# A seven-product stage: VectorE's sum of two banks ahead of a low part, 24 fill matmuls in every unit, and other places for some steps

## The chip, the cores and the metric

The kernel runs on one core of a Trainium2 chip. TensorE (PE in the profile) multiplies into PSUM, VectorE (DVE) and ScalarE (ACT) do the elementwise work, SyncE (SP) issues nearly all the transfers, and GpSimd (POOL) does almost nothing here. Each engine takes its instructions in the order in which they are written. The metric is the device time of one execution in microseconds, as the median of several.

## The reference

Three layers follow each other on 4 x 3072 = 12288 rows of 256 channels:

```python
scores = (1/S) * z @ z.T;  x = u * (relu(scores)**2 @ v)        # z: 64 columns, S = 3072
h = x @ w_in;              x = (h - tanh(h)) @ w_out            # 256 -> 2048 -> 256
xk, xr = a mix of each row of x with the row before it
out = sigmoid(xr @ w_r) * (relu(xk @ w_k)**2 @ w_v)             # 256 -> 1024 -> 256
```

## The kernel before

**Number format.** Every fp32 operand of a matmul is split into a high part (a rounded copy, type fp32r) and a low part (the operand less its high part). A product of two such operands is three matmuls: high by high, high by low, low by high (`PASSES`). `copy_hi` makes a high part on ScalarE, `sub_lo` a low part on VectorE.

**Stages.** The rows are cut into 24 tiles of 512. The program has three stages: A (attention, 24 x 12 units), S (the middle layer, 96 units) and K (the last layer). TensorE runs all of it; the other engines prepare operands and take results out of PSUM.

**Stage S.** Two tiles of rows are taken together as a chunk; there are 12 chunks of 8 units. A unit computes h for two blocks of 128 of the 2048 columns and for both tiles of rows, as a 2x2 block product in seven multiplications instead of eight. The blocks of w_in are A11, A12, A22 and their sums S1 to S4; the blocks of x are B11, B21, B22 and their differences T1 to T4. The seven products go into the two PSUM banks `e` and `a` of a tile `w_H`; there are two such tiles, used in turn. A product is 3 matmuls of 128x512, a unit 21. Between the products `h_unit` puts "fill" matmuls of the second multiplication (by w_out), which belong to an earlier unit and come from a list `q`, in three runs:

1. A11·B11 and A12·B21. ScalarE copies bank `a` (`r`, L628), VectorE adds bank `e` to it (L698). ScalarE makes the high part `h_Hy` of the unit before, VectorE its low part `l_Hy`.
2. Run 1 of the fill. Then S2·T2 and S1·T1. ScalarE copies both banks (`rc`, L628).
3. Run 2 of the fill, then steps that prepare weights or the next chunk's x (`run_steps`). Then high and low part `h_Hx`, `l_Hx` (`h_split`), the products S4·B22 and S3·T3, and VectorE's sum of both banks with the swapped copy (`rc`, L717). Tanh (L632) and h - tanh(h) (L635) follow.
4. Run 3 of the fill. Then -A22·T4 into bank `a`, which the sum L717 has read before. Its tanh is the last step.

The cuts of the list are `len(q) * 8 // 24` and `len(q) * 15 // 24`, so 24 entries go in runs of 8, 7 and 9. `h_queue(n)` lists what the unit after n multiplies. It lists 18 matmuls for the second unit of a chunk, 30 for the first one, and 24 for the others. In the second unit's list the first entries use `h_Hy` and `l_Hy`, which that unit itself makes. At a chunk's end `x2_out` copies four banks of results out (ScalarE, L739).

**Steps.** `run_steps` takes steps from a list of tasks with due units; each step has a cost, and a unit of stage S gives 1.6 to it. What is overdrawn is taken from the next units' budgets. `x_steps(i)` prepares chunk i: four differences T1 to T4 (in two steps of two, L369), the high and low parts of B11 and B21 (one step), of B22, and of T1 to T4. It may start five units before its chunk.

Of the kernel before, what the change touches and what calls it, by code (L numbers as in the profile page):

```python
# [7 lines left out]
F32 = mybir.dt.float32  # L8
# [11 lines left out]
def relu2_attention__tanh_ffn__channel_mix_kernel(  # L20
# [24 lines left out]
    B, S, D = u.shape  # L45
# [5 lines left out]
    NT = B * NG  # L51
# [310 lines left out]
    def x_steps(i):  # L362

        st = {}
        x = xs[i] = {}

        def minus(n, a, b):
            st[n] = t = p2(f"xd{i}_{n}")
            nc.vector.tensor_tensor(out=t, in0=a, in1=b, op=ALU.subtract)  # L369

        def first():
            a, b = [t.bitcast(F32) for t in xraw[i]]
            minus("T1", b[:, 0], a[:, 0])
            minus("T3", b[:, 1], b[:, 0])

        def second():
            a, b = [t.bitcast(F32) for t in xraw[i]]
            minus("T2", b[:, 1], st["T1"])
            minus("T4", st["T2"], a[:, 1])

        def own(k):
            w = xraw[i][k]
            if k:
                copy_hi(w[:, 0], w[:, 1].bitcast(F32))
                sub_lo(w[:, 1], w[:, 1].bitcast(F32), w[:, 0])
                x["B22"] = (w[:, 0], w[:, 1])
            else:
                h = p4(f"xh{i}", F32R)
                copy_hi(h, w.bitcast(F32))
                sub_lo(w, w.bitcast(F32), h)  # L390
                x["B11"], x["B21"] = (h[:, 0], w[:, 0]), (h[:, 1], w[:, 1])

        def part(n):
            t = st.pop(n)
            if i % 2:
                w = sb.tile([P, 2, 512], F32R, tag="e", name=f"xo{i}_{n}", bufs=5)
            else:
                w = p4(f"xo{i}_{n}", F32R)
            copy_hi(w[:, 0], t)
            sub_lo(w[:, 1], t, w[:, 0])  # L400
            x[n] = (w[:, 0], w[:, 1])

        return [(1.3, first), (1.3, second), (1.3, lambda: own(0))] + [
            (0.7, lambda n=n: part(n)) for n in ("T2", "T1")
        ] + [(0.7, lambda: own(1))] + [(0.7, lambda n=n: part(n)) for n in ("T3", "T4")]

# [224 lines left out]
    def tanh(g, h):  # L631
        nc.scalar.activation(out=g, in_=h, func=ACTF.Tanh)  # L632
# [29 lines left out]
    def h_queue(n):  # L662

        i, j = divmod(n, NHF)
        q = h_piece(n - 1, 1, 0) if j else []
        if j == 0:
            return h_piece(n, 0, 1) + h_piece(n, 1, 1) + h_piece(n, 0, 0)
        q += h_piece(n, 0, 0) + h_piece(n, 0, 1) + h_piece(n, 1, 1)
        if j == NHF - 1:
            q += [lambda: x2_out(i, 1)] + h_piece(n, 1, 0) + [lambda: x2_out(i, 0)]  # L670
        return q

    def h_split(which):

# [10 lines left out]
    def h_unit(n, q):  # L685

        i, j = divmod(n, NHF)
        if "g" not in hb:
            g = sb.tile([P, 2, 2, 512], F32, tag="big", name="g_H", bufs=12)
            hb["g"] = [g[:, 0], g[:, 1]]  # L690
        gx, gy = hb["g"]
        cuts = [len(q) * 8 // 24, len(q) * 15 // 24]
        w = work(f"w_H{n}")
        e, a = w[:, 0], w[:, 1]
        product(a, i, j, "A11", "B11", True, False)
        product(e, i, j, "A12", "B21", True, True)
# [12 lines left out]
        rc = copied(scratch(f"rc_{n}"), w)
        for f in q[cuts[0] : cuts[1]]:  # L710
            f()
        run_steps(NA + n)
        hb["x"] = (n, 0 if n else 1, 2, ((n - 1, 1, 0) if n else None, (n, 0, 0)), gx)
        h_split("x")()
        product(e, i, j, "S4", "B22", False, True)
        product(a, i, j, "S3", "T3", False, False)
        nc.vector.tensor_tensor(out=swapped(rc), in0=w, in1=swapped(rc), op=ALU.add)  # L717
        tanh(gy, rc)
        less(gy, rc)
        hb["y"] = (n, 0, 2, ((n, 1, 1), (n, 0, 1)), gy)  # L720
        for f in q[cuts[1] :]:
            f()
        product(a, i, j, "-A22", "T4", False, True)
        tanh(gx[:, 0], a)
        hb["a"] = a
# [9 lines left out]
    def x2_out(i, t):  # L735
        o = acc.pop(("H", 2 * i + t))
        for c in range(DC):
            x = p2(f"x2_{2 * i + t}_{c}")
            nc.scalar.activation(out=x, in_=o[:, c], func=ACTF.Copy)  # L739
            nc.sync.dma_start(out=x2d[2 * i + t][:, c], in_=x)  # L740
            nc.gpsimd.tensor_copy(edge[:, 2 * i + t, c : c + 1], x[:, TB - 1 :])
# [151 lines left out]
        pieces(last + n, min(last + n + 4, NA - 1), 0, k)  # L893
    weights(last + 8, NA, "out", 0)
    weights(NA, NA, "out", 2)
    for k in range(4):
        pieces(NA + k // 2 + 1, NA + 3, 1, k)
    weights(NA + 3, NA + 4, "out", 1)
    weights(NA + 4, NA + 4, "out", 3)
    n = NB - NHF  # L900
    weights(n + 2, n + 3, "r", 0)
# [18 lines left out]
    def run_steps(n):  # L920

        for x in [x for x in tasks if x[1] <= n]:
            tasks.remove(x)
            ready.append((x[0], list(x[3](*x[4]))))
        ready.sort(key=lambda x: x[0])
        kind = units[min(n, len(units) - 1)][0]
        left = {"A": 2.0, "S": 1.6, "K": 2.4, "R": 4.0}[kind] + spare[0]
        if kind == "A":
            t, q = divmod(n, NP)
            j = pairs[t % NG][q] // 2 - t % NG  # L930
            left -= 0.3 if later(n) else 1.0 if j < 0 else 1.1 if j > 0 else 0.0
        while ready and (left > 0 or ready[0][0] <= n):
            for x in list(ready):
                if left > 0 or x[0] <= n:
                    cost, f = x[1].pop(0)
                    f()
                    left -= cost
                    if not x[1]:
                        ready.remove(x)
        spare[0] = min(left, 0.0)  # L940

    with tc.manual_schedule():
        z_load(0, 0)
# [12 lines left out]
        for m, src in ((0, moe2_mu_k), (1, moe2_mu_r)):
            with nc.allow_non_contiguous_dma(reason="a column of the mixing vector"):
                nc.sync.dma_start(out=mu[:, m, :], in_=src.rearrange("(c p) -> p c", p=P))
        def begin(n):
            for f in loads.pop(n, ()):  # L960
                f()
            if n in stores:
                stores.pop(n)()

        for n in range(NA):
            begin(n)
            produce(units[n])
# [58 lines left out]
```

## Time and profile before

| what | value |
|---|---|
| median of 3 runs | 2650.04 us (2649.84 to 2650.11) |
| the profiled execution | 2651.18 us |
| its span, from the first to the last instruction | 2649.1 us |
| instructions in it | 29587 |
| mean granted TensorE clock | 0.991 of full speed |
| busy share of PE, DVE, ACT | 97%, 72%, 60% |

The span is what the trace covers; 2.08 us of the profiled time lie outside it. Matmuls are pipelined: one of 128x512 is shown with some 0.39 us, but the next one starts after 0.23 us, so that two overlap and a window counts those at both of its edges. Weight loads (PEld) run beside matmuls. Units of stage S are named here by their place in the chunk, j = 0 to 7, and matmuls within a unit by their place from its first product, k = 0, 1, ...

### The profile page before, as it was taken

To read this page: it belongs to the slowest core of one execution; us is meant where nothing else is said; L and a number is where in the kernel's file an instruction comes from. 1 tells how busy PE (TensorE), PEld (TensorE's weight loads), DVE (VectorE), ACT (ScalarE), POOL (GpSimd) and SP (SyncE) were. 2 spreads that over 40 slices of the span, in tenths; PEclk is the share of its full clock that TensorE was granted. 3 is DMA by queue.
4 is the path that set the end of the run, shared out by engine and by line. 5 is a ranking of instruction groups with operands and counts; after the bars stand their busy time and mean duration, and the time that the engine had idled before them with its cause. 6 is when DMAs were issued, how large, how long until landed. Compare 5 with 4: busy or idle time off the path is not lost.

```text
span 2649.1 us, 29587 instructions
## 1 busy us (share of the span) xinstructions
PE 2561.3 (97%) x11051; PEld 2082.9 (79%) x11051; DVE 1896.0 (72%) x2363; ACT 1585.6 (60%) x1973; POOL 15.9 (1%) x53
## 2 busy tenths in 40 slices
PE   9999999999999988999999999999998999999999
PEld 7888888888888877777777777777777788888887
DVE  8888888887788676666766676666666666766765
ACT  7766865776687655555555555555555545544553
POOL 0000000000000000000000000000000000000000
PEclk9999999999999999999999999999999999999999
DMA  7798689579868920000000000000010112121121
GB/s 193 224 232 210 200 230 231 178 215 223 209 228 259 219 96 32 1 32 32 1 32 32 32 1 32 32 32 1 32 60 9 48 42 46 40 47 41 43 46 32
DMA packets 382784, 260.17 MB, mean 98 GB/s; under 512 B 263984, under 2 KB 337712, under 8 KB 382640
## 3 DMA queue, kind: packets, MB, share of 16 engines
q1 hardware_dynamic: 379472, 257.89, 35.7%
q8 instruction: 86, 1.41, 0.2%
q10 hardware_dynamic: 3168, 0.39, 0.1%
q14 instruction: 58, 0.48, 0.1%
HBM read 142.87 MB, written 109.31 MB: 95 GB/s over the span
## 4 chain that ended last, share of the span: by engine, by line
PE 79%; DVE 10%; ACT 7%; DMA 1%; issue 1%; SPq 0%; ACTq 0%; DVEq 0%
PE acc_A L607 28%; PE w_H L622 14%; PE acc_H L655 10%; PE w_K L544 10%; PE acc_K L607 10%; DVE rc L717 3%; PE w_A L521 3%; PE w_A L520 3%; DVE l_Hx L90 3%; PE w_R L559 2%; ACT rc L628 2%; ACT h_Hx L87 1%; DVE xd_T L369 1%; DVE g_H L635 1%; ACT x L739 1%
## 5 line engine op out<-in xcount | busy, mean ns | idle before, releaser
L607 PE MATMUL acc_A<-h_A,v 128*128 128x512 f32 x1344 | 440.0, 389 | 0.8 <-DVE h_A L431 0.8
L622 PE MATMUL w_H<-xo_T,w_in 128*128 128x512 f32 x1152 | 327.5, 407 | 36.8 <-DVE rc L717 35.7
L607 PE MATMUL acc_A<-h_t,v 128*128 128x512 f32 x960 | 309.8, 389 | 0.0
L622 PEld LDWEIGHTS w_H<-xo_T,w_in 128*128 128x128 f32 x1152 | 218.2, 194 | 109.7 <-DVE rc L717 66.0
L655 PE MATMUL acc_H<-h_Hy,w_out 128*128 128x512 f32 x768 | 273.8, 400 | 23.9 <-ACT h_Hy L87 23.9
L607 PEld LDWEIGHTS acc_A<-h_A,v 128*128 128x128 f32 x1344 | 252.2, 188 | 53.7 <-DVE h_A L431 1.2
L427 ACT ACTIVATE a_A<-w_A 128x1024 f32<-128x1024 f32 (+1 forms) x169 | 172.7, 1022 | 198.8 <-PE w_A L521 198.1
L607 PE MATMUL acc_A<-l_A,v 128*128 128x512 f32 x672 | 261.8, 390 | 2.3 <-DVE l_A L90 2.3
L632 ACT ACTIVATE g_H<-rc 128x1024 f32<-128x1024 f32 x96 | 101.8, 1061 | 257.6 <-DVE rc L717 257.6
L655 PE MATMUL acc_H<-h_Hx,w_out 128*128 128x512 f32 x768 | 254.1, 389 | 0.0
L607 PE MATMUL acc_K<-h_K,w_v 128*128 128x512 f32 x768 | 251.8, 389 | 0.0
L544 PE MATMUL w_K<-mkh,w_k 128*128 128x512 f32 x768 | 249.0, 390 | 0.0
L90 DVE TENSOR_TENSOR l_A<-a_A,h_A 128x1024 fp32r<-128x1024 f32 (+1 forms) x169 | 201.9, 1194 | 65.7 <-ACT h_A L87 64.8
L427 ACT ACTIVATE a_K<-w_K 128x1024 f32<-128x1024 f32 x96 | 98.2, 1023 | 225.2 <-PE w_K L544 225.2
L455 DVE STREAM_TRANSPOSE k<-a_A 128x512 f32<-128x512 f32 x240 | 156.0, 689 | 76.4 <-ACT a_A L428 75.8
L607 PEld LDWEIGHTS acc_A<-h_t,v 128*128 128x128 f32 x960 | 180.2, 188 | 37.4
L635 DVE TENSOR_TENSOR g_H<-rc,g_H 128x1024 f32<-128x1024 f32 x96 | 117.7, 1226 | 114.2 <-ACT g_H L632 114.2
L90 DVE TENSOR_TENSOR l_Hx<-g_H,h_Hx 128x1024 fp32r<-128x1024 f32 (+1 forms) x97 | 117.6, 1212 | 113.2 <-ACT h_Hx L87 113.2
L431 DVE CAST h_K<-a_K 128x1024 fp32r<-128x1024 f32 x96 | 66.5, 693 | 184.3 <-ACT a_K L428 181.5
L628 ACT ACTIVATE rc<-w_H 128x1024 f32<-128x1024 f32 x96 | 98.7, 1028 | 163.4 <-PE w_H L622 163.4
L655 PEld LDWEIGHTS acc_H<-h_Hy,w_out 128*128 128x128 f32 x768 | 148.6, 194 | 59.8 <-ACT h_Hy L87 29.0
L607 PE MATMUL acc_A<-l_t,v 128*128 128x512 f32 x480 | 186.7, 389 | 0.0
(154 smaller groups left out, 5081.7 us busy)
## 6 DMA issues: line engine op xcount, KB each, us to landing
at<-k SPq DMA_DIRECT2D x120, 512.0 KB, 3.6
b<-at SPq DMA_DIRECT2D x240, 256.0 KB, 6.3
vr<-in_v_dram SPq DMA_DIRECT2D x24, 512.0 KB, 7.1
uin<-in_u_dram SPq DMA_DIRECT2D x192, 64.0 KB, 2.7
x1d<-x SPq DMA_DIRECT2D x24, 512.0 KB, 3.3
x<-x1d SPq DMA_DIRECT2D x24, 512.0 KB, 4.7
x2d<-x SPq DMA_DIRECT2D x48, 256.0 KB, 2.3
x<-x2d SPq DMA_DIRECT2D x24, 512.0 KB, 3.3
```

The lines of the kernel that those rows point to most:

```text
L90: nc.vector.tensor_tensor(out=o, in0=i, in1=hi.bitcast(F32), op=ALU.subtract)
L427: nc.scalar.activation(out=a[:, x], in_=w[:, x], func=ACTF.Relu, scale=sc)
L455: nc.vector.transpose(out=t[:, :, :, c].rearrange("p b a j -> p a b j"), in_=a[:, c].rearrange("p (a b i) -> p a b i", a=4, b=4),)
L520: nc.tensor.matmul(w[:, j], lhsT, z1[b, g], start=True, stop=False)
L521: nc.tensor.matmul(w[:, j], lhsT, z2[t], start=False, stop=True)
L544: nc.tensor.matmul(w[:, j], ws["k", f // 4][a][:, c, (f % 4) * P : (f % 4 + 1) * P], x[m][:, c], start=n == 0, stop=n == 3 * DC - 1,)
L607: nc.tensor.matmul(o[c], w[j][a][:, c * P : (c + 1) * P], s[m][:, j], start=p == 0 and j == 0 and n == 0, stop=p == last and j == 1 and n ...
L622: nc.tensor.matmul(o, w[l][:, (j % 4) * P : (j % 4 + 1) * P], x[m], start=first and k == 0, stop=last and k == 2, skip_group_check=True,)
L628: nc.scalar.activation(out=t, in_=a, func=ACTF.Copy)
L632: nc.scalar.activation(out=g, in_=h, func=ACTF.Tanh)
L635: nc.vector.tensor_tensor(out=g, in0=h, in1=g, op=ALU.subtract)
L655: nc.tensor.matmul(o[c], ws["out", f // 4][a][:, f % 4, c * P : (c + 1) * P], hp[n, half, t][m], start=bool(first and k == 0), stop=bool(l ...
```

## The change

The sum of both banks (L717) is written ahead of the low part `l_Hx`. The fill is cut at 6 and 14 of 24, so in runs of 6, 8 and 10. The lists of the first two units of a chunk are filled up to 24: the last six matmuls of a chunk move into the second unit of the next one, and `x2_out` is called from the list, one tile in the first unit and one in the second. The first unit of the stage gets 18, since six of its 24 move to the second. The differences T1 to T4 become four steps, a unit's budget falls from 1.6 to 1.4, and the weight pieces of the first chunk get other units.

```diff
-        def first():
-            a, b = [t.bitcast(F32) for t in xraw[i]]
-            minus("T1", b[:, 0], a[:, 0])
-            minus("T3", b[:, 1], b[:, 0])
...
+        def sums():
+            b21, b11, b22, b12 = raw()
+            return [
+                (0.7, lambda: minus("T1", b12, b11)),
+                (0.7, lambda: minus("T3", b22, b12)),
+                (0.7, lambda: minus("T2", b22, st["T1"])),
+                (0.7, lambda: minus("T4", st["T2"], b21)),
+            ]
...
-        return [(1.3, first), (1.3, second), (1.3, lambda: own(0))] + [
+        return sums() + [(1.3, lambda: own(0))] + [
...
     def h_queue(n):
 
         i, j = divmod(n, NHF)
-        q = h_piece(n - 1, 1, 0) if j else []
+        q = h_piece(n - 1, 1, 0) if n else []
         if j == 0:
-            return h_piece(n, 0, 1) + h_piece(n, 1, 1) + h_piece(n, 0, 0)
-        q += h_piece(n, 0, 0) + h_piece(n, 0, 1) + h_piece(n, 1, 1)
+            if n:
+                q[-1] = with_out(q[-1], i - 1, 0)
+            return q + h_piece(n, 0, 1) + h_piece(n, 1, 1) + h_piece(n, 0, 0)
         if j == NHF - 1:
-            q += [lambda: x2_out(i, 1)] + h_piece(n, 1, 0) + [lambda: x2_out(i, 0)]
-        return q
+            q += h_piece(n, 0, 1) + h_piece(n, 1, 1) + h_piece(n, 0, 0)
+            q[17] = with_out(q[17], i, 1)
+            return q
+        return q + h_piece(n, 0, 0) + h_piece(n, 0, 1) + h_piece(n, 1, 1)
+
+    outs = []
+
+    def with_out(f, i, t):
+        def g():
+            f()
+            outs.append((i, t))
+
+        return g
+
+    def empty():
+        for x in outs:
+            x2_out(*x)
+        outs.clear()
...
-        cuts = [len(q) * 8 // 24, len(q) * 15 // 24]
+        cuts = [len(q) * 6 // 24, len(q) * 14 // 24]
...
-        h_split("x")()
+        low = h_split("x")
+        empty()
         product(e, i, j, "S4", "B22", False, True)
         product(a, i, j, "S3", "T3", False, False)
         nc.vector.tensor_tensor(out=swapped(rc), in0=w, in1=swapped(rc), op=ALU.add)
+        low()
+        for f in q[cuts[1] :]:
+            f()
+        empty()
         tanh(gy, rc)
         less(gy, rc)
         hb["y"] = (n, 0, 2, ((n, 1, 1), (n, 0, 1)), gy)
-        for f in q[cuts[1] :]:
-            f()
...
-    for k in range(4):
-        pieces(NA + k // 2 + 1, NA + 3, 1, k)
-    weights(NA + 3, NA + 4, "out", 1)
+    for k, n in enumerate((NA + 1, NA + 2, NA + 3, NA + 2)):
+        pieces(n, n, 1, k)
+    weights(NA + 4, NA + 4, "out", 1)
...
-        left = {"A": 2.0, "S": 1.6, "K": 2.4, "R": 4.0}[kind] + spare[0]
+        left = {"A": 2.0, "S": 1.4, "K": 2.4, "R": 4.0}[kind] + spare[0]
...
         q = [f for u in units[NA - LAG : NA] for f in pieces_of(u)]
-        q += [f for cost, f in x1_steps(NT - 1)]
+        rest = q[-6:] + [f for cost, f in x1_steps(NT - 1)]
+        q = q[:-6]
         for n in range(NS):
             begin(NA + n)
             h_unit(n, q)
-            q = h_queue(n)
+            q = rest + h_queue(n)
+            rest = []
+        q += h_piece(NS - 1, 1, 0)
+        q[-1] = with_out(q[-1], NT // 2 - 1, 0)
```

First place, VectorE in unit 26 (j = 2 of a chunk); `l_Hy25` belongs to the unit before. Before:

```order
L698 TENSOR_TENSOR r1_26_10273<-w_H26_10266,r1_26_10273 128x512
L635 TENSOR_TENSOR g_H_8381<-w_H25_10200,g_H_8381 128x512
L90 TENSOR_TENSOR l_Hy25_10277<-g_H_8381,h_Hy25_10276 128x1024
L635 TENSOR_TENSOR g_H_8381<-r1_26_10273,g_H_8381 128x512
L90 TENSOR_TENSOR l_Hx26_10307<-g_H_8381,h_Hx26_10306 128x1024
L717 TENSOR_TENSOR rc_26_10297<-w_H26_10266,rc_26_10297 128x2x512
L635 TENSOR_TENSOR g_H_8381<-rc_26_10297,g_H_8381 128x1024
```

And now, with the lines of the changed file (L718, L638 and L738 are the old L698, L635 and L717):

```order
L718 TENSOR_TENSOR r1_26_10273<-w_H26_10266,r1_26_10273 128x512
L638 TENSOR_TENSOR g_H_8379<-w_H25_10186,g_H_8379 128x512
L90 TENSOR_TENSOR l_Hy25_10277<-g_H_8379,h_Hy25_10276 128x1024
L638 TENSOR_TENSOR g_H_8379<-r1_26_10273,g_H_8379 128x512
L738 TENSOR_TENSOR rc_26_10295<-w_H26_10266,rc_26_10295 128x2x512
L90 TENSOR_TENSOR l_Hx26_10306<-g_H_8379,h_Hx26_10305 128x1024
L638 TENSOR_TENSOR g_H_8379<-rc_26_10295,g_H_8379 128x1024
```

The sum `rc_26` and the low part `l_Hx26` have changed places. Second place, TensorE between the second and the third product of the same unit, `xo3_T2` and `xo3_T1` being T2 and T1 of its chunk. Before:

```order
L622 MATMUL w_H26_10266<-xh3_9871,w_in0_0_7415 128x512
L655 MATMUL acc_H6_10251<-h_Hx25_10237,w_out2_8418 128x512
L655 MATMUL acc_H6_10251<-l_Hx25_10238,w_out2_8418 128x512
L655 MATMUL acc_H6_10251<-h_Hx25_10237,w_out2_8418 128x512 x2
L655 MATMUL acc_H6_10251<-l_Hx25_10238,w_out2_8418 128x512
L655 MATMUL acc_H6_10251<-h_Hx25_10237,w_out2_8418 128x512
L655 MATMUL acc_H6_10251<-h_Hx25_10237,w_out0_8374 128x512
L655 MATMUL acc_H6_10251<-l_Hx25_10238,w_out0_8374 128x512
L622 MATMUL w_H26_10266<-xo3_T2_9940,w_in0_1_7786 128x512 x3
```

And now:

```order
L625 MATMUL w_H26_10266<-xh3_9936,w_in0_0_7415 128x512
L658 MATMUL acc_H6_10249<-h_Hx25_10226,w_out2_8411 128x512
L658 MATMUL acc_H6_10249<-l_Hx25_10227,w_out2_8411 128x512
L658 MATMUL acc_H6_10249<-h_Hx25_10226,w_out2_8411 128x512 x2
L658 MATMUL acc_H6_10249<-l_Hx25_10227,w_out2_8411 128x512
L658 MATMUL acc_H6_10249<-h_Hx25_10226,w_out2_8411 128x512
L625 MATMUL w_H26_10266<-xo3_T2_9939,w_in0_1_7786 128x512 x3
```

Two fill matmuls fewer stand ahead of S2·T2. Third place, TensorE at the same spot of unit 25 (j = 1), where `h_Hy24` and `l_Hy24` are made in unit 25 itself and `h_Hx24` in unit 24. Before:

```order
L655 MATMUL acc_H7_10217<-h_Hy24_10210,w_out0_8374 128x512
L655 MATMUL acc_H7_10217<-l_Hy24_10211,w_out0_8374 128x512
L655 MATMUL acc_H7_10217<-h_Hy24_10210,w_out0_8374 128x512 x2
L655 MATMUL acc_H7_10217<-l_Hy24_10211,w_out0_8374 128x512
L655 MATMUL acc_H7_10217<-h_Hy24_10210,w_out0_8374 128x512
L622 MATMUL w_H25_10200<-xo3_T2_9940,w_in0_1_7786 128x512 x3
```

And now:

```order
L658 MATMUL acc_H4_9674<-h_Hx24_10151,w_out3_8708 128x512
L658 MATMUL acc_H4_9674<-l_Hx24_10152,w_out3_8708 128x512
L658 MATMUL acc_H4_9674<-h_Hx24_10151,w_out3_8708 128x512 x2
L658 MATMUL acc_H4_9674<-l_Hx24_10152,w_out3_8708 128x512
L658 MATMUL acc_H4_9674<-h_Hx24_10151,w_out3_8708 128x512
L625 MATMUL w_H25_10186<-xo3_T2_9939,w_in0_1_7786 128x512 x3
L625 MATMUL w_H25_10186<-xo3_T1_10008,w_in0_1_7786 128x512 x3
L658 MATMUL acc_H7_10217<-h_Hy24_10196,w_out0_8374 128x512
```

Six matmuls on the parts of the unit before last (`acc_H4`, the chunk before) stand first, and the first use of `h_Hy24` comes after S2·T2 and S1·T1 instead of ahead of them.

## Rows read from the trace of the kernel before

**Rows 1.** The page, chain that ended last: shares of the span by engine.

```profile
PE 79%; DVE 10%; ACT 7%; DMA 1%; issue 1%; SPq 0%; ACTq 0%; DVEq 0%
```

**Rows 2.** Windows of stages A and S: length, PE, PEld, DVE, ACT, POOL, clock, DMA, GB/s.

```profile
0.00:943.42 943.42, 937.07 (x4115) 773.46 (x4116) 770.58 (x1084) 669.53 (x765) 0.73 (x5) 1.00 0.81 217
943.42:1039.63 96.21, 85.22 (x355) 68.12 (x354) 67.29 (x75) 53.68 (x68) 0.00 (x0) 0.96 0.11 38
1039.63:1950.50 910.87, 858.55 (x3601) 681.30 (x3600) 597.70 (x660) 505.99 (x661) 12.41 (x40) 0.98 0.07 24
1950.50:2030.52 80.02, 73.58 (x317) 58.66 (x316) 51.67 (x54) 45.89 (x59) 1.24 (x4) 1.00 0.15 56
2030.52:2058.28 27.76, 24.14 (x100) 19.49 (x99) 16.93 (x19) 15.17 (x23) 0.08 (x1) 0.94 0.00 1
```

**Rows 3.** Windows of units j = 0, 1, 2, 4 of one chunk, same columns.

```profile
1678.58:1690.17 11.59, 11.59 (x53) 9.57 (x52) 7.06 (x8) 6.33 (x10) 0.00 (x0) 1.00 0.00 0
1690.17:1704.88 14.71, 11.58 (x41) 8.22 (x40) 6.24 (x7) 6.75 (x11) 1.24 (x4) 0.88 0.39 143
1704.88:1715.09 10.21, 10.21 (x47) 8.45 (x46) 6.61 (x7) 5.91 (x8) 0.00 (x0) 1.00 0.01 2
...
1725.96:1737.08 11.12, 10.51 (x47) 8.37 (x46) 7.74 (x8) 6.61 (x9) 0.00 (x0) 1.00 0.00 0
```

**Rows 4.** Waits of TensorE in stage S: us in total, times, longest.

```profile
PE w_H L622 <- DVE rc L717: 35.7, 47, 3.6
PE acc_H L655 <- ACT h_Hy L87: 23.9, 12, 2.0
PE acc_H L655 <- DVE l_Hy L90: 12.5, 12, 1.4
```

**Rows 5.** Timeline of that j = 1 unit: start, us, [idle before <-releaser].

```profile
1689.68 2.04 ACT L739 ACTIVATE x<-acc_H 128x512 f32<-128x512 f32 x4
...
1693.69 0.50 PE L655 MATMUL acc_H<-h_Hy,w_out 128*128 128x512 f32 x1 [2.02 <-ACT h_Hy L87]
...
1697.06 2.54 PE L622 MATMUL w_H<-xo_T,w_in 128*128 128x512 f32 x6
```

**Rows 6.** Timeline of unit j = 5 of that chunk, at its last product.

```profile
1746.01 1.22 DVE L717 TENSOR_TENSOR rc<-w_H,rc 128x1024 f32<-128x1024 f32 x1
...
1746.38 0.39 PE L655 MATMUL acc_H<-h_Hy,w_out 128*128 128x512 f32 x1
1747.28 0.53 PEld L622 LDWEIGHTS w_H<-xo_T,w_in 128*128 128x128 f32 x3 [0.94 <-DVE rc L717]
...
1748.08 0.40 PE L622 MATMUL w_H<-xh,w_in 128*128 128x512 f32 x1
```

**Rows 7.** Timeline of unit j = 2 of that chunk, its first half.

```profile
1704.85 0.39 PE L622 MATMUL w_H<-xh,w_in 128*128 128x512 f32 x1
...
1706.42 0.60 ACT L628 ACTIVATE r<-w_H 128x512 f32<-128x512 f32 x1 [0.71 <-PE w_H L622]
...
1707.05 0.69 DVE L698 TENSOR_TENSOR r<-w_H,r 128x512 f32<-128x512 f32 x1 [0.65 <-ACT r L628]
...
1708.04 1.52 PE L622 MATMUL w_H<-xo_T,w_in 128*128 128x512 f32 x6
1708.26 1.22 DVE L90 TENSOR_TENSOR l_Hy<-g_H,h_Hy 128x1024 fp32r<-128x1024 f32 x1
...
1709.60 1.03 ACT L628 ACTIVATE rc<-w_H 128x1024 f32<-128x1024 f32 x1 [1.11 <-PE w_H L622]
```

**Rows 8.** Timeline of the first chunk's last unit, at its last product.

```profile
1038.84 0.50 PE L622 MATMUL w_H<-xo_T,w_in 128*128 128x512 f32 x1 [3.62 <-DVE rc L717]
```

**Rows 9.** Timeline of stage K at the first product by w_r.

```profile
2072.02 0.69 DVE L776 CAST mkh<-mxk 128x1024 fp32r<-128x1024 f32 x1
2072.16 0.50 PE L559 MATMUL w_R<-mrl,w_r 128*128 128x512 f32 x1 [2.39 <-DVE mrl L90]
2072.62 0.74 DVE L769 SCALAR_TENSOR_TENSOR mxr<-x,head,mxr 128x512 f32<-128x512 f32 x1
```

More of the change, by code (lines that the diff above doesn't have):

```diff
@@ L369, in minus, with raw @@
             nc.vector.tensor_tensor(out=t, in0=a, in1=b, op=ALU.subtract)
-        def first():
+        def raw():
             a, b = [t.bitcast(F32) for t in xraw[i]]
-            minus("T1", b[:, 0], a[:, 0])
-            minus("T3", b[:, 1], b[:, 0])
-        def second():
-            a, b = [t.bitcast(F32) for t in xraw[i]]
-            minus("T2", b[:, 1], st["T1"])
-            minus("T4", st["T2"], a[:, 1])
+            return a[:, 1], a[:, 0], b[:, 1], b[:, 0]
+        def sums():
[6 more added lines that the diff above has]
+            ]
         def own(k):
@@ L992, in relu2_attention__tanh_ffn__channel_mix_kernel @@
                     f()
+                empty()
             elif n < len(units) + LAG:
```

## The prediction

> **What bounds the kernel now.** I read the chain that ended last first: 79% of the span is TensorE, 10% VectorE, 7% ScalarE [rows 1]. So TensorE sets the time, and the rest is time in which it waits. The windows by stage say where: stage A has TensorE busy for 937.07 of 943.42 us, while stage S (943.42 to 2058.28, so 1114.86 us) is busy for less, at a granted clock of 0.94 to 1.00 [rows 2]. Then the units of one chunk. The j = 2 unit shows the pace: 45 matmuls (the window counts two at its edges) in 10.21 us, never idle, so 0.227 us each [rows 3]. The j = 0 unit is no worse: 51 matmuls in 11.59 us. The j = 1 unit has 39, which at that pace are 8.85 us, but it takes 14.71 us at a mean clock of 0.88. Units like j = 4 have 45 and take 11.12 us. Ninety-six units at 10.21 us would be 980 us; some 130 us are lost.
>
> The waits name the two losses [rows 4]. In j = 1 the fill asks for `h_Hy` and `l_Hy` before ScalarE and VectorE have made them, 12 times each. That wait is followed by six matmuls that take 2.54 us [rows 5], where an undisturbed unit needs 1.52 us [rows 7]: the lower of the two clock levels, 1.2 instead of 2.4 GHz. In the others -A22·T4 waits for the sum L717 (47 times), which stands behind the steps and behind `l_Hx`.
>
> **What a late operand costs.** In the j = 5 unit [rows 6] the last fill starts at 1746.38, so -A22·T4 was due at 1746.61. The sum ends at 1747.23, 0.62 us late. The next unit starts at 1748.08 instead of 1746.61 + 3 x 0.227 = 1747.29, so 0.79 us late: a wait costs its lateness and 0.17 us more, since the weight load starts only with the release (1747.28). An operand must therefore be there 0.17 us before its product is due. Against that row stands a rule of the Trainium skill, page "TensorE: Matmul & The Clock Gate", Part 3, "The mechanism": TensorE pulls weight loads ahead of matmuls in flight. By it the 0.17 us would be hidden; the row shows that they are not for a product that waits on a bank. The rival below has the sum for it.
>
> **The change, in a unit without steps.** Times from the unit's first product, read off [rows 7], the pace 0.227.
> - Run 1 shrinks from 8 to 6, so S2·T2 moves from k = 14 (due 3.18) to k = 12 (due 2.72). It waits for VectorE's addition to `r`, which hangs on the first two products alone and does not move: it ends at 1707.05 + 0.69 - 1704.85 = 2.89. Before, 2.89 + 0.17 = 3.06 is in time, and the row has S2·T2 at 3.19. Now it is late: 2.89 - 2.72 + 0.17 = **0.34 us, in every unit**. This is the new wait, and everything behind it moves by 0.34.
> - The sum L717 no longer stands behind `l_Hx`. S3·T3 ends with k = 31: 31 x 0.227 + 0.34 + 0.39 = 7.77, the sum runs 7.8 to 9.0, and -A22·T4 (k = 42) is due at 9.87, so 9.70 would do. No wait. `l_Hx` (1.22) then runs to 10.2, and its first reader is a fill matmul of the next unit, k = 7: free. The tanh of the sum starts no later than before, so `h_Hy` is not later either.
> - With steps: the heaviest normal unit makes B11 and B21 and one T. ScalarE's `rc` ends at 5.66, a copy of such a size (1.03) at 6.6 to 6.7, VectorE's low part (1.22) at 7.9, the T's (0.69) at 8.5 to 8.6, the sum at 9.6 to 9.8. On the edge: I take 0, with 0.15 us a chunk as the bound. The other steps end earlier. So the 0.9 us that j = 4 and its like lose [rows 3] go.
> - Units j = 0 and 1 now ask for `l_Hy` at k = 19, due 4.31 + 0.34 = 4.65; it ends at 1708.26 + 1.22 - 1704.85 = 4.63: 0.15 us late, against some 4 us and the clock in j = 1 before. The others ask at k = 25, 1 us after it is there.
> - `x2_out`: four copies of 2.04 us stood between the tanh of the sum and the next unit's `r` [rows 5]. Now two of 1.0 stand ahead of the tanh in j = 0 and two in j = 1. Their bank is complete with k = 35 (8.7), so the tanh starts at 9.7 instead of 9.0 and h - tanh(h) ends near 12.0, 1.5 us into the next unit. ScalarE makes `h_Hy` only after `r`, at 2.2. Free.
> - Transfers: the order on SyncE's queue changes at the stage's start and by one load near its end, each load a unit or more ahead of use. Nothing.
>
> So a unit is 10.21 + 0.34 = 10.55 us, a chunk 8 x 10.55 + 0.3 = 84.7 us.
>
> **The sum.**
> - Ten middle chunks: 910.87 -> 847 + 0.7 (in one of them five steps fall into j = 7, VectorE 0.7 late) = 848: **-62.9**.
> - First chunk: its first unit has 39 matmuls, 8.85, with S2·T2 at k = 10 (late 0.79) and the sum 0.2 late: 9.85. Five units of 10.55 and 0.15: 52.9. Unit 4 makes two weight parts one after the other, 0.45 late: 11.0. Unit 7 waits 3.62 us now [rows 8]: it gets ten steps instead of eight (2 x 0.69 more) and loses `l_Hx` (1.22) ahead of the sum, so that wait stays and the unit is 14.2. Sum 88.0 against 96.21: **-8.2**.
> - Last chunk but its last unit: 7 x 10.55 + 0.3 + 0.45 = 74.6 against 80.02: **-5.4**.
> - The stretch 2030.52 to 2058.28 holds 99 matmuls, 22.5 us, + 0.34 + a sum that stands behind four mixing steps instead of five and not behind `l_Hx`, 1.4 late (before 3.6): 24.2 against 27.76: **-3.6**.
> - Stage K: the split of the mixing work puts two casts (0.69) and a mixing instruction (0.74) ahead of `mrl`, for which TensorE waits 2.39 us [rows 9]: with their overlap **+1.9**.
> - Clock: the waits of j = 1 go, and with them most of the low level; for the two long waits that stay (3.6 and 4.3 us) I add **+1.5**, between 0 and 3.4.
>
> Together -76.7. The profiled execution (span 2649.1, 2651.18 with 2.08 outside) goes to 2574.5; it stands 1.1 us above the median 2650.04, which goes to **2573 us**.
>
> **Rivals.**
> - *The addition is in time or the weights are loaded ahead.* S2·T2 writes bank `a`, and the addition reads bank `e`. Were only the copy to `r` waited for (1706.42 + 0.60 - 1704.85 = 2.17), the 0.34 would vanish: 96 x 0.34 = 33 us less, 2540. If only the 0.17 vanished (the page's rule above, by a mechanism of this kernel: the weights wait in the array while the bank is read), 16 us less, 2557. For it: nothing in these rows, since in all of them S2·T2 comes after the addition; against it [rows 6], where the weight load starts with the release.
> - *The clock still falls once a chunk.* One fall in j = 1 is 14.71 x 0.12 = 1.8 us lost [rows 3]. Eleven of them: 2573 + 19 = 2592. For it: waits still follow each other in j = 0 and 1 (0.34 and 0.15). Against it: j = 4 is late by 0.9 us at clock 1.00.
> - *The copies hold the tanh.* If the bank is released only with the unit's last product (10.8), the tanh of j = 0 ends at 12.9, h - tanh(h) at 14.1, and S2·T2 of j = 1 is late by 1.6 instead of 0.34 us: 1.3 us eleven times, and eleven times more if j = 1 holds its copies likewise: 2587 to 2602. Against it: the copies in [rows 5] start at 1689.68, half a us before the next unit does [rows 3], so before -A22·T4 is through.
> - *Small waits that I don't see*, 0.2 to 0.5 us a unit: 2592 to 2621.
> - *Slower than before.* Every unit now has a wait. If such waits kept TensorE at its lower level, a matmul would start every 0.45 us, and each us there costs half of one; the gain of 77 us is eaten when 154 us, 13 a chunk, are spent there. Against it: j = 4 again, and ten chunks at 0.98 though five units in eight wait. The skill's same page, "Why this matters for your kernels", speaks for this rival in so far as it advises against idle gaps between bursts of matmuls because they bring the clock down; its rows are about longer gaps than 0.34 us.
> - *No change*: TensorE would have to lose elsewhere all that it wins; no row shows where.
>
> **How the numbers follow.** Forecast 0.60 (own range 2563 to 2585); addition or weights in time 0.04 and 0.07; clock 0.10; copies 0.07; small waits 0.08; slower 0.03; no change 0.01. The range 2553 to 2600 leaves out the 2540 case, most of the small waits and the last two: some 0.15. Within 0.2% (5 us, about what a measurement of this kernel can tell from no change) I put 0.02, slower 0.03, faster 0.95.
>
> **What would show it.** Right: windows of 10.5 to 10.6 us for middle units, TensorE's wait for the sum L738 down to the unit 7 kind, a new wait of the weight load of w_H for the addition L718 in nearly all 96 units, S2·T2 at 3.1 us, j = 1 near 10.7 us at clock 1.00, `mrl` awaited for over 4 us. Wrong: no wait at S2·T2 (2540); j = 1 over 12 us or a clock of 0.98 in the middle chunks; ScalarE's x2 copies ending after -A22·T4.

## The result, and the profile after

| what | before | after |
|---|---|---|
| median | 2650.07 us (2649.84 to 2651.52, 4 runs) | 2579.72 us (2577.64 to 2580.78, 4 runs) |
| the profiled execution, its span | 2651.18, 2649.1 us | 2580.78, 2578.8 us |
| mean granted TensorE clock | 0.991 | 0.997 |

The ratio is 0.9732, with a 95% interval of 0.9716 to 0.9749. The forecast was 2573 us; the time lies 6.7 us above it, inside the range.

The page of the changed kernel, its chain of work that ended last, as in [rows 1]:

```profile
PE 90%; DVE 4%; ACT 3%; DMA 1%; issue 1%; SPq 0%; ACTq 0%; DVEq 0%
```

VectorE and ScalarE have gone from 17% of that chain to 7%. The windows of the changed kernel by stage (columns as in [rows 2]): stage A, the first chunk, the second, the next nine, the last chunk without its last unit, the stretch to stage K, stage K.

```profile
0.00:944.88 944.88, 938.15 (x4116) 774.28 (x4116) 769.85 (x1083) 668.79 (x764) 0.73 (x5) 1.00 0.81 216
944.88:1033.45 88.57, 84.29 (x356) 65.94 (x355) 68.31 (x77) 54.64 (x69) 0.00 (x0) 0.99 0.14 45
1033.45:1120.08 86.63, 85.61 (x362) 67.39 (x361) 58.78 (x66) 50.79 (x66) 1.39 (x4) 0.99 0.08 25
1120.08:1884.50 764.42, 759.09 (x3241) 601.11 (x3240) 537.21 (x596) 460.01 (x595) 12.54 (x36) 1.00 0.07 25
1884.50:1959.30 74.80, 74.11 (x316) 58.34 (x315) 51.43 (x55) 46.16 (x58) 1.39 (x4) 1.00 0.17 60
1959.30:1983.45 24.15, 22.82 (x99) 18.25 (x99) 15.47 (x18) 14.35 (x20) 0.27 (x1) 1.00 0.00 0
1983.45:2578.80 595.35, 585.61 (x2570) 483.95 (x2569) 392.55 (x474) 295.99 (x404) 1.19 (x4) 0.99 0.19 43
```

All that was won lies in stage S: 1038.57 us against 1114.86. A usual chunk takes 764.42 / 9 = 84.94 us (forecast 84.7). Stage K has become 4.5 us longer and stage A 1.5 us. The units j = 0, 1, 2 and 5 of chunk 8, as in [rows 3]:

```profile
1629.67:1640.41 10.74, 10.64 (x46) 8.29 (x45) 6.26 (x7) 6.47 (x9) 1.02 (x2) 1.00 0.04 14
1640.41:1651.12 10.71, 10.66 (x46) 8.29 (x45) 6.92 (x8) 6.87 (x10) 0.37 (x2) 1.00 0.35 119
1651.12:1661.69 10.57, 10.51 (x47) 8.37 (x45) 6.60 (x8) 5.70 (x7) 0.00 (x0) 1.00 0.18 67
...
1682.82:1693.44 10.62, 10.51 (x46) 8.37 (x45) 7.86 (x9) 6.99 (x9) 0.00 (x0) 1.00 0.01 2
```

Every unit of this chunk now has 45 matmuls, and the clock of j = 1 is 1.00 instead of 0.88. The long units are gone, but the short one has gone too: j = 2 took 10.21 us and takes 10.57. The waits of TensorE's weight loads in stage S say why. [rows 4] has the waits of the matmuls behind these loads, so the last line here is the weight loads' wait for the sum in the kernel before:

```profile
PEld w_H L625 <- DVE r L718: 47.9, 96, 0.9
PEld w_H L625 <- DVE rc L738: 7.7, 6, 3.6
PEld acc_H L658 <- DVE l_Hy L90: 6.2, 23, 0.3
...
PEld w_H L622 <- DVE rc L717: 66.0, 70, 4.0
```

The wait for the sum has fallen from 70 times to 6 (as waits of matmuls from 47 to 5), that for `h_Hy` has no row left, and a new one for VectorE's addition stands in each of the 96 units. The timeline of unit j = 2, which begins at 1651.12 (compare [rows 7]):

```profile
1652.68 0.60 ACT L631 ACTIVATE r<-w_H 128x512 f32<-128x512 f32 x1 [0.76 <-PE w_H L625]
1653.31 0.69 DVE L718 TENSOR_TENSOR r<-w_H,r 128x512 f32<-128x512 f32 x1 [1.29 <-ACT r L631]
...
1654.06 1.22 PEld L625 LDWEIGHTS w_H<-xo_T,w_in 128*128 128x128 f32 x6 [0.48 <-DVE r L718]
1654.06 1.65 PE L625 MATMUL w_H<-xo_T,w_in 128*128 128x512 f32 x6
...
1659.01 1.23 DVE L738 TENSOR_TENSOR rc<-w_H,rc 128x1024 f32<-128x1024 f32 x1 [2.68 <-PE w_H L625]
```

The addition ends 1653.31 + 0.69 - 1651.12 = 2.88 us into the unit, the forecast had 2.89. The sum starts at 7.9, behind its product and not behind `l_Hx`, as forecast.

### The profile page after: what moved, and what is told of

It reads as the page before. It is cut to its first block, busy times and chain, and to the rows that moved or that the text cites. A ratio compares the mean times of both kernels' runs of the same rounds, so it can differ in the third digit from the quotient of the medians.

```text
span 2578.8 us, 29584 instructions
## 1 busy us (share of the span) xinstructions
PE 2549.7 (99%) x11051; PEld 2069.3 (80%) x11051; DVE 1893.6 (73%) x2363; ACT 1590.7 (62%) x1973; POOL 17.5 (1%) x53
## 4 chain that ended last, share of the span: by engine, by line
PE 90%; DVE 4%; ACT 3%; DMA 1%; issue 1%; SPq 0%; ACTq 0%; DVEq 0%
PE acc_A L610 29%; PE w_H L625 19%; PE acc_H L658 15%; PE w_K L547 10%; PE acc_K L610 10%; PE w_A L524 3%; PE w_A L523 3%; PE w_R L562 3%; DVE r L718 3%; ACT r L631 2%; DMA b<-at 1%; DMA zin<-in_z_dram 0%; SPq L105 0%; DVE rc L738 0%; DVE xo_T L90 0%
## 5 line engine op out<-in xcount | busy, mean ns | idle before, releaser
L625 PE MATMUL w_H<-xo_T,w_in 128*128 128x512 f32 x1152 | 322.1, 401 | 12.7 <-DVE rc L738 5.3
L625 PEld LDWEIGHTS w_H<-xo_T,w_in 128*128 128x128 f32 x1152 | 208.5, 188 | 95.0 <-DVE r L718 47.9
L658 PE MATMUL acc_H<-h_Hx,w_out 128*128 128x512 f32 x768 | 268.1, 390 | 0.0
L658 PE MATMUL acc_H<-h_Hy,w_out 128*128 128x512 f32 x768 | 252.7, 390 | 0.0
L738 DVE TENSOR_TENSOR rc<-w_H,rc 128x1024 f32<-128x1024 f32 x96 | 117.4, 1223 | 135.4 <-PE w_H L625 135.4
L635 ACT ACTIVATE g_H<-rc 128x1024 f32<-128x1024 f32 x96 | 101.9, 1062 | 168.7 <-DVE rc L738 168.7
L431 ACT ACTIVATE a_A<-a_A 128x1024 f32<-128x1024 f32 (+1 forms) x169 | 178.4, 1056 | 5.4
L87 ACT ACTIVATE h_t<-b 128x512 fp32r<-128x512 f32 x240 | 136.7, 619 | 65.0 <-PE acc_A L610 48.3
L658 PEld LDWEIGHTS acc_H<-h_Hx,w_out 128*128 128x128 f32 x768 | 144.2, 188 | 30.7
```

What stands on the lines that cost most here:

```text
L87: nc.scalar.activation(out=o, in_=i, func=ACTF.Copy)
L431: nc.scalar.activation(out=a[:, x], in_=a[:, x], func=ACTF.Square)
L625: nc.tensor.matmul(o, w[l][:, (j % 4) * P : (j % 4 + 1) * P], x[m], start=first and k == 0, stop=last and k == 2, skip_group_check=True,)
L658: nc.tensor.matmul(o[c], ws["out", f // 4][a][:, f % 4, c * P : (c + 1) * P], hp[n, half, t][m], start=bool(first and k == 0), stop=bool(l ...
```

## Experiments

The kernel before, run beside these, had medians of 2650.4 to 2652.8 us.

**How the new wait grows: three cuts.** Units j = 2 to 7 of the changed kernel get another cut, j = 0 and 1 keep 6 and 14. The first:

```diff
-        cuts = [len(q) * 6 // 24, len(q) * 14 // 24]
+        c = (6, 14) if j < 2 else (8, 15)
+        cuts = [len(q) * k // 24 for k in c]
```

> The changed kernel, with the fill of units j = 2 to 7 cut at 8 and 15 of 24 again, and at 6 and 14 only in j = 0 and 1. Theory of the prediction (S2·T2 waits 0.34 us for VectorE's addition because it is due at k = 12): at k = 14 it is due at 3.18, the addition is there at 2.89 + 0.17 = 3.06, so the wait goes in six units of eight; they take 10.21 us instead of 10.57. The sum L738 of the heaviest unit (j = 5) ends at 9.64 and is now due at 9.53 - 0.17 = 9.36, so that unit keeps 0.3 to 0.4 us. 72 x 0.36 less, 12 x 0.37 back: about -21 us, 2558 us (2552 to 2565). Rival (the 0.34 us is a price of the unit as such, for instance of the alternation of the two accumulations, or the wait goes to the next reader, rc or the sum): units stay at 10.5, 2575 to 2583 us.

Measured: 2557.96 us, ratio 0.9647 (0.9629 to 0.9665). The second has `(7, 15)` in that line:

> The same with cuts at 7 and 15 in units j = 2 to 7. S2·T2 is due at k = 13, 2.95 us, and the addition ends at 2.89, so it is in time by 0.06 us. Theory of the prediction (a wait costs the lateness and 0.17 us more, since the weight load starts with the release): 0.11 us remain, units of 10.32 us, and in j = 5 some 0.2 us for the sum: 72 x 0.25 less, 2 us back, about -16 us, 2564 us. Rival (weights are loaded ahead, so only lateness counts): units of 10.21 us, as with cuts at 8 and 15, about 2558 us or less. The window of a middle unit tells the two apart, 10.32 against 10.21.

Measured: 2564.40 us, ratio 0.9670 (0.9652 to 0.9688). The third has `(4, 14)`:

> The same with cuts at 4 and 14 in units j = 2 to 7: S2·T2 is due at k = 10, 2.27 us. Theory: late by 2.89 - 2.27 + 0.17 = 0.79 us, units of 11.0 us instead of 10.57, 72 x 0.43: +31 us, 2611 us, and the granted clock stays at 1.00 in these units. Rival (a fixed price for any such wait): 2580 us. Rival (waits of 0.8 us in each unit bring the clock down): above 2630 us, with a granted clock under 0.98 over the middle chunks.

Measured: 2608.48 us, ratio 0.9837 (0.9819 to 0.9855). The windows of the j = 2 unit, at 8 with that of j = 5 behind it, and at 8 and 7 the first weight load of S2·T2. Cut at 8:

```profile
1635.62:1645.82 10.20, 10.20 (x46) 8.45 (x45) 6.38 (x8) 5.70 (x7) 0.00 (x0) 1.00 0.19 68
1666.22:1676.81 10.59, 10.52 (x46) 8.37 (x45) 7.98 (x9) 6.88 (x9) 0.00 (x0) 1.00 0.01 2
...
1638.57 1.32 PEld L625 LDWEIGHTS w_H<-xo_T,w_in 128*128 128x128 f32 x6
1638.80 1.52 PE L625 MATMUL w_H<-xo_T,w_in 128*128 128x512 f32 x6
```

at 7:

```profile
1639.85:1650.18 10.33, 10.33 (x46) 8.37 (x45) 6.37 (x8) 5.69 (x7) 0.00 (x0) 1.00 0.19 67
...
1642.04 0.69 DVE L719 TENSOR_TENSOR r<-w_H,r 128x512 f32<-128x512 f32 x1 [1.29 <-ACT r L631]
1642.78 1.22 PEld L625 LDWEIGHTS w_H<-xo_T,w_in 128*128 128x128 f32 x6 [0.25 <-DVE r L719]
```

at 4, with the window of its nine middle chunks behind it:

```profile
1668.92:1679.92 11.00, 10.49 (x46) 8.37 (x45) 6.60 (x8) 5.69 (x7) 0.00 (x0) 1.00 0.18 60
1121.86:1910.24 788.38, 758.63 (x3242) 601.27 (x3240) 537.45 (x596) 459.85 (x595) 12.50 (x36) 1.00 0.07 25
```

With 8, 7, 6 and 4 entries in run 1 the unit takes 10.20, 10.33, 10.57 and 11.00 us. S2·T2 comes due 0.227 us earlier with each entry that run 1 loses, and from 7 to 4 entries the unit grows by 0.67 us, where 3 x 0.227 is 0.68. At 7 the addition ends 0.07 us before S2·T2 is due (2.95), and 0.13 us are lost all the same. With the addition at 2.88 in all of them, the price beyond the lateness is 0.13 + 0.07 = 0.20 us at 7, 0.37 - 0.16 = 0.21 at 6, and 0.80 - 0.61 = 0.19 at 4: the 0.17 of [rows 6], a little larger. The Trainium skill, page "TensorE: Matmul & The Clock Gate", Part 3, "The mechanism", has weight loads pulled ahead of matmuls in flight, where they go to other rows of the array or to the background weight buffer. Where the release comes in time, the trace agrees: at 8 the load of S2·T2 starts 0.23 us ahead of its product, beside a fill matmul. At 7 it is the load itself that waits: it starts 0.05 us behind the end of the addition, and its lead is gone. That the price of some 0.2 us is this lead is an argument from these rows; no run parts it. At 4 each of six units in eight loses 0.80 us, and the clock stays at 1.00 over nine chunks, against the rival that such waits bring it down. At 8 the wait that has gone uncovers the next one in j = 5, 0.39 us for the sum.

**What the early cut is for.** The changed kernel with one cut for all:

```diff
-        cuts = [len(q) * 6 // 24, len(q) * 14 // 24]
+        cuts = [len(q) * 8 // 24, len(q) * 15 // 24]
```

> The changed kernel with cuts at 8 and 15 in all units, j = 0 and 1 too. There the seventh and eighth entry of the fill use h_Hy and l_Hy, which the unit itself makes: h_Hy ends at 3.1 us and is due at k = 12, 2.72; l_Hy ends at 4.63 and is then due at 3.5. Theory: two waits of together 1.85 us in each of j = 0 and 1, units of 12.1 us, against 21 us won in the other six: 2580 - 21 + 22 x 1.35 = 2589 us, and up to 2608 us if the clock falls once in each chunk as it did before. Rival (the early cut costs 0.34 us in each unit and buys nothing): 2580 - 33 = 2547 us.

Measured: 2587.03 us, ratio 0.9758 (0.9736 to 0.9779). The waits of the weight loads in stage S:

```profile
PEld acc_H L658 <- DVE l_Hy L90: 29.0, 22, 1.3
PEld acc_H L658 <- ACT h_Hy L87: 15.8, 22, 0.7
```

j = 0 and 1 take 12.1 us there instead of 10.7, at a clock of 1.00 over the middle chunks. So the early cut pays in two units of eight and costs 0.36 us in the others; as one number for all it is 7 us better than 8 and 22 us worse than two numbers.

**The place of the sum.** First the changed kernel with the low part ahead of the sum again:

```diff
-        low = h_split("x")
+        h_split("x")()
...
-        low()
```

> The changed kernel with VectorE's low part l_Hx written ahead of the sum L738 again, all else as changed. Theory: only units whose steps need ScalarE or much of VectorE pay. In j = 5 l_Hx would run from 8.4 to 9.6 and the sum end at 10.8 where 9.70 is wanted: 1.1 us. In j = 6 and 7 h_Hx ends at 7.65, l_Hx at 8.9, the sum at 10.0: 0.3 us each. No loss in j = 0 to 4. Some 1.7 us a chunk, 12 chunks, and 2 us at the stage's ends: +23 us, 2603 us (2595 to 2612). Rival (the steps, made smaller and spread, removed the waits by themselves, the place of the sum is worth nothing): 2580 us. Rival (the place of the sum is all of it, 3.6 us a chunk): 2623 us.

Measured: 2605.63 us, ratio 0.9830 (0.9813 to 0.9846). The window of unit j = 5:

```profile
1697.99:1709.62 11.63, 10.79 (x46) 8.29 (x45) 8.02 (x9) 6.86 (x9) 0.00 (x0) 1.00 0.01 1
```

It loses 1.0 us against 10.62; in the middle chunks j = 6 and 7 lose 0.3 to 0.4 each, the others nothing. Then the kernel before, with the same reorder alone:

```diff
-        h_split("x")()
+        low = h_split("x")
         product(e, i, j, "S4", "B22", False, True)
         product(a, i, j, "S3", "T3", False, False)
         nc.vector.tensor_tensor(out=swapped(rc), in0=w, in1=swapped(rc), op=ALU.add)
+        low()
```

> The kernel before, with one change: the sum L717 is written ahead of l_Hx. Theory: units j = 3 to 7 lose 0.3 to 0.95 us each to this wait, 3.6 us a chunk; the sum then starts 1.14 us earlier and is in time in all of them, while j = 0 and 1 stay as they are: 2650 - 42 = 2608 us. Rival (steps of 1.3 at a budget of 1.6 still hold the sum, so that the smaller steps are needed): 2625 us or more.

Measured: 2613.47 us, ratio 0.9858 (0.9843 to 0.9873), 5 us above my figure. In the middle chunks the five units did go to 10.20 to 10.23 us, but j = 0 became longer. Its window:

```profile
1651.33:1664.58 13.25, 11.86 (x53) 9.50 (x51) 7.72 (x8) 7.16 (x10) 0.87 (x2) 1.00 0.06 22
```

and the one wait of TensorE's weight loads in it:

```profile
PEld acc_H L655 <- DVE l_Hx L90: 1.8, 1, 1.8
```

It took 11.59 [rows 3]. Its list of 30 ends with six matmuls on the `h_Hx` and `l_Hx` that this unit itself makes, and with the reorder `l_Hx` starts 10.0 us into the unit instead of 7.2. I had read the list for j = 1 and not for j = 0. This loses 1.66 us in each of eleven chunks, 18 us; most of it does not show in the total, since j = 1 became 7 us shorter over the ten middle chunks and the first chunk 7.1 us shorter instead of 3.6, neither of which I had forecast. The changed kernel is spared this, since there those six stand in the next unit.

**The even lists alone.** The kernel before with the lists, `x2_out` and the start of the stage as changed (the diff of `h_queue`, `with_out`, `empty` and `rest` as in the change), cut at 6 and 14 in j = 0 and 1 and at 8 and 15 elsewhere; the sum, the steps and the budget as before:

> The kernel before, with the lists of 24 matmuls in every unit alone (x2_out called from the list, cuts at 6 and 14 in j = 0 and 1 and at 8 and 15 in the other units); the sum L717 stays behind l_Hx, the steps and their budget stay. Theory: j = 0 and 1 together go from 26.3 us (13.2 to 17.3 for j = 1) to 21.4 with no low clock, -4.9 us in each of eleven chunks and somewhat more in the first: 2590 us (2585 to 2598); j = 3 to 7 keep their 3.6 us a chunk. Rival (only the low clock, 22 us of stage S, goes, and the wait for h_Hy and l_Hy moves elsewhere): 2628 us.

Measured: 2597.52 us, ratio 0.9797 (0.9783 to 0.9812); 7 us above my figure. j = 1 and j = 4 of a chunk:

```profile
1652.12:1662.84 10.72, 10.67 (x47) 8.29 (x45) 7.03 (x8) 6.86 (x10) 0.88 (x2) 1.00 0.35 116
1683.91:1695.07 11.16, 10.56 (x47) 8.37 (x46) 7.74 (x8) 6.63 (x9) 0.00 (x0) 1.00 0.00 0
```

In the middle chunks j = 0 and 1 together take 21.48 us in place of 24.7 to 27.0, and j = 4 keeps its loss.

**Both, with the steps as before.** That kernel and the reorder:

```diff
-        h_split("x")()
+        low = h_split("x")
         empty()
...
+        low()
```

> The kernel before with both: the lists of 24 with cuts at 6 and 14 in j = 0 and 1 and 8 and 15 elsewhere, and the sum ahead of l_Hx; steps of two differences, the budget of 1.6 and the old places of the first weight pieces stay. Theory (the two gains are apart from each other): 2650 - 42 - 58 = 2550 us, and the mixing steps of stage K are less late than in the changed kernel (a wait of 2.4 us for mrl, and no fall of the clock there). Rival (the smaller steps are needed to keep the sum in time once the 0.34 us wait is gone): units j = 3 to 6 wait up to 0.5 us each, 2565 us or more.

Measured: 2549.29 us, ratio 0.9616 (0.9602 to 0.9631). In the middle chunks units j = 2 to 7 all take 10.20 to 10.23 us, so the smaller steps, the smaller budget and the moved weight pieces of the change are not needed for the sum; against `cut8_late_units`, which has them, it is 8.7 us faster. Of the 8.0 us between the two profiled spans some 3.5 are j = 5 of nine chunks, 2.6 the first two chunks, and 1.7 stage K.

**Why S2·T2 waits at all.** It writes bank `a`; the addition reads bank `e`. The changed kernel with two tiles (the pool of the banks is changed at the stage's ends):

```diff
-        w = work(f"w_H{n}")
-        e, a = w[:, 0], w[:, 1]
+        e, a = [wk[0].tile([P, 512], F32, tag=x, name=f"{x}_H{n}", bufs=2) for x in ("we", "wx")]
         product(a, i, j, "A11", "B11", True, False)
+        r1 = copied(p2(f"r1_{n}"), a)
         product(e, i, j, "A12", "B21", True, True)
-        r1 = copied(p2(f"r1_{n}"), a)
...
         product(a, i, j, "S2", "T2", False, False)
+        rc = scratch(f"rc_{n}")
+        copied(rc[:, 1], a)
         product(e, i, j, "S1", "T1", True, False)
-        rc = copied(scratch(f"rc_{n}"), w)
+        copied(rc[:, 0], e)
...
-        nc.vector.tensor_tensor(out=swapped(rc), in0=w, in1=swapped(rc), op=ALU.add)
+        nc.vector.tensor_tensor(out=rc[:, 1], in0=e, in1=rc[:, 1], op=ALU.add)
+        nc.vector.tensor_tensor(out=rc[:, 0], in0=a, in1=rc[:, 0], op=ALU.add)
```

> The changed kernel (runs of 6, 8 and 10 in all units), in which the two banks of a unit of stage S are two tiles of their own instead of one tile of two banks; the copy of bank a is written ahead of the second product, rc is copied and the sum made bank by bank (two instructions of 512 each instead of one of 1024). S2·T2, which writes bank a, then asks for ScalarE's copy of bank a alone, and S1·T1, which writes bank e, for VectorE's addition. Theory (the 0.34 us is there because the two banks are one tile, so that S2·T2 is held by a reader of the other bank): the copy runs 0.9 to 1.5, the addition 1.6 to 2.3, S2·T2 is due at 2.72 and S1·T1 at 3.4, so no wait; l_Hy of j = 0 and 1 ends near 4.0 instead of 4.63 and is in time at 4.31 - 0.17. All units at 10.2 to 10.3: 96 x 0.34 + 22 x 0.15 = 36 us less, up to 4 us back where the tiles of one stage give way to those of the next: 2546 us (2541 to 2553). Rival (the smaller instructions, 0.1 us more of ScalarE and 0.06 of VectorE in a unit, or the change of the order make the sum or rc late): some units above 10.4, 2555 us or more. Rival (the wait is not one for the other bank): 2575 to 2585 us.

Measured: 2541.59 us, ratio 0.9591 (0.9578 to 0.9604). The timeline of its unit j = 2, which begins at 1621.23 (`wx` is bank `a`):

```profile
1622.11 0.60 ACT L643 ACTIVATE r<-wx_H 128x512 f32<-128x512 f32 x1
...
1622.86 0.69 DVE L729 TENSOR_TENSOR r<-we_H,r 128x512 f32<-128x512 f32 x1 [1.26 <-PE we_H L637]
...
1623.95 0.84 PE L637 MATMUL wx_H<-xo_T,w_in 128*128 128x512 f32 x3
```

The copy starts 0.88 us into the unit instead of 1.56, the addition ends at 2.32 instead of 2.88, and S2·T2 starts at 2.72, when it is due. With the addition as early as that, S2·T2 would be in time in one tile too. The stage's first unit tells more. There VectorE has other work first and the addition is late, and run 1 has four entries, so S2·T2 is due at 945.57. The last line is S2·T2 of the same unit in the changed kernel:

```profile
945.50 0.69 DVE L729 TENSOR_TENSOR r<-we_H,r 128x512 f32<-128x512 f32 x1
945.57 0.84 PE L637 MATMUL wx_H<-xo_T,w_in 128*128 128x512 f32 x3
946.25 0.53 PEld L637 LDWEIGHTS we_H<-xo_T,w_in 128*128 128x128 f32 x3 [0.26 <-DVE r L729]
...
947.82 1.23 PEld L625 LDWEIGHTS w_H<-xo_T,w_in 128*128 128x128 f32 x6 [0.94 <-DVE r L718]
```

With two tiles S2·T2, into bank `a`, starts on time, 0.62 us before the addition ends; only S1·T1, into bank `e`, waits for it. With one tile S2·T2 waits. So the 0.34 us was there because both banks were kept in one tile: the writer of one bank waited for the reader of the other. Why the copy of bank `a` comes earlier the run doesn't part: it is now written ahead of the second product as well as reading a tile of its own. By the times of the changed kernel two tiles alone should do, since its copy ends at 2.16, before S2·T2 is due, and its addition at 2.88, before S1·T1 is due at 3.40; that is an estimate, and no run has them alone.

> The kernel of the run old_steps_best (cuts at 6 and 14 in j = 0 and 1, 8 and 15 elsewhere, sum ahead of the low part, steps as before) with the same two tiles. There only j = 0 and 1 still wait, 0.53 us each. Theory: both at 10.2 to 10.3, 23 x 0.5 = 12 us less, up to 4 us back at the ends of the stage: 2549 - 10 = 2539 us (2535 to 2545). Rival (the wait goes to l_Hy alone and stays 0.5 us): 2549 to 2553 us.

Measured, with the edit above made to the kernel of `old_steps_best`: 2538.00 us, ratio 0.9579 (0.9565 to 0.9592), the fastest of all. Beside it that kernel again:

> The kernel of the run old_steps_best once more, in five rounds and beside the one with two tiles: 2549 us (2546 to 2552).

Measured: 2549.52 us, ratio 0.9622 (0.9608 to 0.9635). With two tiles and the steps as before, stage S takes 1001.0 us, where its 4369 matmuls at 0.227 would take 992; of the rest, 2.0 us are a new wait of stage K's first product for the stage's last elementwise step. Its row stands in the two runs with changed pools and in no other.

## Why the prediction was right, and where its sum was off

| term | forecast | measured |
|---|---|---|
| a unit without steps | 10.55 us | 10.57 |
| j = 0 and j = 1 | 10.70 each | 10.75, 10.71 |
| ten middle chunks | -62.9 | -59.8 |
| first chunk | -8.2 | -7.6 |
| last chunk but its last unit | -5.4 | -5.2 |
| stretch to stage K | -3.6 | -3.6 |
| stage K | +1.9 | +4.5 |
| stage A | 0 | +1.5 |
| clock, apart | +1.5 | lies in the rows above |
| sum | -76.7 | -70.3 |

**The pace and the new wait** stand, the wait by its place, its releaser and, to 0.02 us, its price. The 0.17 us of one row was 0.19 to 0.21 in the cuts, and that 0.02 in some eighty units, with 0.05 in j = 0, makes 2.1 of the 3.1 us by which the middle chunks fall short. S2·T2 was to start at 3.1; its record starts at 2.94, with the release, and its matmuls and those of S1·T1, six together, then take 1.65 us instead of 1.52: part of the price lies in the group and not ahead of it.

**The sum ahead of `l_Hx`**, forecast with no wait in a usual unit, had none in 90 of 96 units, and `l_Hx` cost its next reader nothing, which holds only together with the even lists, as `sum_first_only` showed. **The heavy unit** cost 0.05, bound 0.15. **`x2_out`** was free: no row has a wait for `h_Hy`.

**The term that failed is the clock, +1.5 us between 0 and 3.4.** The windows of the changed kernel at the first chunk's last unit, the unit behind it and stage K's first products by w_r; the last row is from the start of stage A:

```profile
1018.72:1033.44 14.72, 11.44 (x46) 8.78 (x45) 13.23 (x18) 9.36 (x13) 0.00 (x0) 0.95 0.00 0
1033.44:1045.06 11.62, 11.60 (x46) 8.97 (x45) 6.29 (x7) 6.47 (x9) 1.02 (x2) 0.92 0.03 13
1994.60:2004.60 10.00, 5.99 (x15) 4.39 (x15) 7.51 (x9) 1.95 (x4) 0.00 (x0) 0.67 0.14 52
...
5.00:15.00 10.00, 7.41 (x24) 5.16 (x23) 9.12 (x15) 7.55 (x10) 0.00 (x0) 0.83 0.92 214
```

The lower of the two levels is half of the full one, so a stretch loses at most its length times what its clock lacks: 0.7 us in unit 7 and 0.9 in the unit behind it. In stage K that bound is 3.3 us; its waits grew by 1.6 us (below) and its length by 4.5, which leaves 2.9 for the clock. Read directly, the thirteen matmuls from 1999.23 to 2004.87 take 5.64 us instead of 13 x 0.227 = 2.95, which is 2.7 more. Together the clock cost 4.5 us instead of 1.5. In stage K the forecast was one wait of 4.3 us for `mrl`; it came as two, with one matmul between them:

```profile
1996.93 0.47 PE L562 MATMUL w_R<-mrh,w_r 128*128 128x512 f32 x1 [2.17 <-DVE mrh L799]
1999.23 0.79 PE L562 MATMUL w_R<-mrl,w_r 128*128 128x512 f32 x1 [1.84 <-DVE mrl L90]
```

Their 4.01 us fit (2.39 before, [rows 9]); what follows at the low level was priced too low. The lateness comes with the smaller steps and budget and the moved weight pieces, as a group: without them `old_steps_best` waits 2.4 us there, once, and its stage K takes 592.4 us. How much low clock follows such a wait differs between executions. These are the ten us that begin with that one wait, in `old_steps_best` and in `old_steps_again`, the same kernel:

```profile
1966.25:1976.25 10.00, 7.61 (x27) 6.09 (x27) 6.65 (x8) 2.44 (x3) 0.00 (x0) 0.83 0.17 53
1967.40:1977.40 10.00, 7.61 (x34) 6.23 (x34) 6.64 (x8) 2.43 (x3) 0.00 (x0) 1.00 0.15 53
```

Stage K takes 592.4 us in the first and 590.9 in the second. Behind the two waits of the changed kernel, `sum_after_low` and `cut8_late_units` have 0.83 and the others 0.66 to 0.69. So no one figure would have held for this term, and no row tells which of them an execution will show. For the 1.5 us of stage A the change shows no cause: the code of its start is the same, the clock there was 0.83 in this execution and 1.00 before, which is at most 1.7 us over those 10, and 5 of the 13 profiled executions have such a low stretch, among them `sum_first_only`, whose stage A is that of before.

So of the 6.4 us between the sum and the span 3.0 are the clock, 2.1 the units and 1.5 stage A; the other rows give 0.2 back.

The rivals: *the addition is in time* fell with the wait for the addition in all 96 units. `two_tiles` made its condition true by an edit and won 38 us, where 33 was worked out: 10.57 to 10.20 us is 0.37 and not 0.34 a unit, and j = 0 and 1 won some 0.5 each. That its 2542 us lie so near the 2540 of that rival is luck, since the forecast behind the 2540 was 6.7 us low. *The weights are loaded ahead* fell with the run cut at 7. *The clock falls once a chunk* and *slower* fell with 1.00 over nine chunks. *Copies hold the tanh* fell with j = 0 and 1 at 10.7 us, *small waits* with a middle unit 0.02 us above its forecast, and *no change* with the time.

## What to carry to other kernels

Read off when each operand is there and when its product is due, both from the unit's start, before moving a cut: one number for all units made six of eight wait for what only two needed. When an engine's instruction is put later, look for its earliest reader in every kind of unit, not in the usual one. Two banks that are written and read at different times should be two tiles, so that a wait for one isn't a wait for both.

## What the runs showed of the hardware

A product that waits on a bank pays some 0.2 us beyond its lateness, even where the release comes 0.07 us before it is due: its weight load, which otherwise starts 0.23 us ahead of it, starts only with the release. A loss of 0.80 us in each unit, six units running, left the granted clock at 1.00 for nine chunks (`cut4_late_units`), while two waits of 2.2 and 1.8 us with one matmul between them stand in a stretch of 10 us at a mean of 0.66 to 0.69 in five runs and of 0.83 in two. One wait of 2.4 us was followed by 1.00 in one execution of a kernel and by 0.83 in another.
